# Pooled attention and two MLPs on one core: weights' signs taken by a parametric relu, key and value batches prepared in ten steps

## The chip, the cores and the metric

One core of one Trainium2 chip runs the whole kernel. The metric is the device time of one execution in microseconds (us). TensorE is called PE below, VectorE DVE, ScalarE ACT, GpSimd POOL, and SP is the queue of SyncE, which issues most DMAs. Each engine takes its instructions strictly in order.

## What is computed

```python
# q, k, v: (8, 8, 576, 64);  w_in: (512, 2048), w_out: (2048, 512), twice
k_p = k.reshape(B, H, 72, 8, D).mean(axis=3)
v_p = v.reshape(B, H, 72, 8, D).mean(axis=3)
scores = q @ k_p.T / sqrt(D)
attn = softmax(scores);  x = attn @ v_p            # 4608 tokens of 512
h = x @ moe_w_in                                    # MLP 1
g = where(h >= 1, h, where(h <= -1, 0, (h + 1)**2 / 4))
x = g @ moe_w_out
h = x @ moe2_w_in                                   # MLP 2
return (h * sigmoid(h)) @ moe2_w_out
```

The arrays come as 64-bit floats. The kernel reads them as pairs of 32-bit words (a low and a high word) and makes 32-bit floats of the weights itself.

## The kernel before

Products are made of float16 pairs (a high and a low half of each operand, three matmuls a product). The 4608 tokens are cut into nine token tiles of 512. MLP 1 runs tile by tile: 16 steps `s` in a tile, each with 12 matmuls for a chunk of h (`emit_h`), a chain on ACT and DVE that makes g (`pre_A`, `min_A`, `mid_A`, `post_A`, `split_g`), and the products with w_out (`yA`). MLP 2 runs afterwards, when all else is done.

Around this main loop there are four kinds of side work.

- **First attention.** The first 128-token blocks (0 to 3) are done in 32-bit floats before the main loop (`stages`); MLP 1 of token tile 0 can't start before.
- **Weights of MLP 1.** w_in comes in nine pieces of up to 256 columns (`weight_in`: `load`, `look`, `scales`, `work`), w_out in eight halves of four column blocks d (`weight_out`). A piece is looked at for its largest entry (`look`), gets a scale (`w_scale`), and is converted: the exponent bits are shifted by 3, the sign is put in, the low word's top bits are put in, it is multiplied by the scale, cut to float16, and the rest is made by a subtraction on POOL. In the kernel before, ACT's Abs with a factor 2^-112 makes the positive high word, one DVE instruction floors it and accumulates the maximum (L248, L190), one shifts (L93), one ORs the sign in (L267 for w_in, L202 for w_out), one ORs the low bits in (L270, L208). Tile 0 runs while its own weights are still being converted.
- **Weights of MLP 2** (`weight_whole`) are converted the same way during tiles 1 to 7.
- **Attention of the later blocks** runs in slots (`att_slots`), four for each block of 128 tokens: one or two slots a step. For each batch of 576 tokens keys and values are prepared: half of each is loaded through SP (`kv_load`), the other half is added by an accumulating DMA that POOL issues (`kv_more`), DVE adds the quarters (`kv_pool`, L459 and L462), ACT takes the mean magnitude (L465), then the sums are scaled, split, and the keys are transposed by two DMAs on SP (`kT<-rows`, L502). The queries of each block go through the same kind of tile (`rows`, two buffers) and a transposing DMA (`qT<-rows`, L554).

The instruction order of each engine is made by a scheduler that runs a model of the timeline; `tc.issue_after` and the helpers `behind` and `paced` hold work back behind an anchor instruction. In the kernel before the sums of a batch are spread evenly over the slots (`pool_to`), and `batches` makes keys and values in the slot of the block that needs them first.

## Time and profile before

| | us |
|---|---|
| median of 3 runs | 1641.39 (1640.28 to 1647.74) |
| the profiled execution | 1640.59 |
| its span, first to last instruction | 1638.8 |

Stretches by what runs in them, in us from the span's start (the boundaries are the first splits of tile 0's last block and the first stores of the outputs of tiles 0, 1, 3 and 8):

| stretch | what runs |
|---|---|
| 0 to 48.3 | first attention; w_in is loaded, its first pieces looked at |
| 48.3 to 134 | tile 0: h and g; w_in converted, the first column block of w_out converted |
| 134 to 209.5 | tile 0: products with w_out; the other three blocks of w_out converted; attention of tile 1 |
| 209.5 to 334.2 | tile 1, two attention slots a step at first |
| 334.2 to 525.7 | tiles 2 and 3 |
| 525.7 to 959.2 | tiles 4 to 8 |
| 959.2 to 1638.8 | MLP 2 |

A window's row gives the busy time of each engine in it, with the number of instructions, then the granted share of PE's clock, the mean share of the 16 DMA engines and their rate. A row of waits gives who waited for whom, the time in total, how often, and the longest. A row of a group gives line, engine, operation, names and shapes, count, then busy time and the mean duration in ns.

### The profile page before, as it was taken

Reading aid. Unit: us, or ns where it says so; the run is one execution under the profiler, and the core shown is the slowest. Engines: PE = TensorE matmul, PEld = TensorE weight load, DVE = VectorE, ACT = ScalarE, POOL = GpSimd, SP = SyncE. Lnnn points to the kernel's source line nnn. Section 1 sums busy time; section 2 is a strip of 40 time slices with the busy share of each in tenths; the row PEclk is TensorE's granted clock in tenths of the full one; section 3 lists DMA queues with packets and bytes.
Section 4 is the critical chain, followed back from the end, with each engine's and each line's share of the span. In section 5 each row is a group of like instructions: output and inputs, shape, how many; then the busy total and the mean of one; then the engine's idle time right before and its main releaser. Section 6 shows DMA issues by size and latency. Waiting matters only on the chain.

```text
span 1638.8 us, 34439 instructions
## 1 busy us (share of the span) xinstructions
PE 1534.5 (94%) x14278; PEld 1052.6 (64%) x14278; DVE 1208.5 (74%) x2166; ACT 894.1 (55%) x1418; POOL 581.8 (36%) x507
## 2 busy tenths in 40 slices
PE   6765889799999999999999999999999999999998
PEld 5322434344444444444444479999999999999998
DVE  6898868566777687787767767777776777777765
ACT  4477455455666556574566555554444544455543
POOL 2342513113343332331355424433333433343322
PEclk9876899899999999999999999999999999999999
DMA  9573688927547366255574330001100000000000
GB/s 295 123 181 86 122 165 190 186 73 130 145 107 166 89 111 138 81 140 163 194 302 145 148 129 28 27 27 32 36 27 28 27 34 34 27 27 28 27 15 27
DMA packets 226157, 166.35 MB, mean 102 GB/s; under 512 B 154960, under 2 KB 193616, under 8 KB 226000
## 3 DMA queue, kind: packets, MB, share of 16 engines
q1 hardware_dynamic: 216592, 155.88, 35.4%
q0 software_dynamic: 9408, 8.27, 3.7%
q8 instruction: 112, 1.84, 0.5%
q14 instruction: 45, 0.37, 0.1%
HBM read 102.76 MB, written 33.55 MB: 83 GB/s over the span
## 4 chain that ended last, share of the span: by engine, by line
PE 50%; DVE 16%; DMA 9%; issue 9%; ACT 9%; POOL 6%; SPq 1%; DVEq 0%; POOLq 0%; ACTq 0%
PE y L120 5%; PE y L122 5%; PE y L121 5%; PE hps L120 4%; PE hps L122 4%; PE hps L121 4%; PE y L1024 4%; PE y L1025 4%; PE y L1026 4%; PE hb L122 4%; PE hb L121 4%; PE hb L120 4%; POOL c L724 4%; DMA kT<-rows 3%; DMA yin<-y 2%
## 5 line engine op out<-in xcount | busy, mean ns | idle before, releaser
L121 PE MATMUL hb<-xl,wc 128*128 128x128 f16 x2016 | 347.6, 219 | 0.0
L122 PE MATMUL hb<-xh,wc 128*128 128x128 f16 x2016 | 347.6, 219 | 0.0
L120 PE MATMUL hb<-xh,wc 128*128 128x128 f16 x2016 | 347.6, 219 | 0.0
L368 DVE SCALAR_TENSOR_TENSOR g<-c,tsg,g 128x512 f16<-128x512 f32 x252 | 228.7, 910 | 97.8 <-ACT g L367 97.8
L1024 PE MATMUL y<-wd,g 128*128 128x256 f16 x1008 | 274.7, 273 | 1.9 <-DVE ob L1037 1.8
L1026 PE MATMUL y<-wd,g 128*128 128x256 f16 x1008 | 274.7, 273 | 0.0
L1025 PE MATMUL y<-wd,g 128*128 128x256 f16 x1008 | 274.7, 273 | 0.0
L120 PE MATMUL hps<-xh,wa 128*128 128x512 f16 x576 | 222.7, 387 | 36.2 <-ACT wa L275 19.7
L964 ACT ACTIVATE c<-c,tc 128x512 f32<-128x512 f32 x144 | 103.2, 717 | 230.8 <-DVE c L961 230.8
L367 ACT ACTIVATE g<-c,tsg 128x512 f16<-128x512 f32 x252 | 177.6, 718 | 85.8 <-POOL c L727 48.3
L122 PE MATMUL hps<-xh,wa 128*128 128x512 f16 x576 | 220.7, 384 | 3.8 <-POOL wa L276 3.8
L121 PE MATMUL hps<-xl,wa 128*128 128x512 f16 x576 | 222.8, 387 | 0.4 <-DVE xl L368 0.2
L120 PE MATMUL y<-g,wb 128*128 128x512 f16 x544 | 210.0, 388 | 11.6 <-ACT wb L220 9.8
L122 PE MATMUL y<-g,wb 128*128 128x512 f16 x544 | 210.6, 387 | 4.7 <-POOL wb L221 4.7
L121 PE MATMUL y<-g,wb 128*128 128x512 f16 x544 | 210.7, 387 | 0.5 <-DVE g L863 0.5
L121 PEld LDWEIGHTS <-wc 128*128 128x128 f16 x2016 | 197.3, 98 | 2.4
L120 PEld LDWEIGHTS <-wc 128*128 128x128 f16 x2016 | 197.3, 98 | 2.2
L122 PEld LDWEIGHTS <-wc 128*128 128x128 f16 x2016 | 197.3, 98 | 0.0
L961 DVE TENSOR_TENSOR c<-c,hb 128x512 f32<-128x512 f32 x252 | 167.8, 681 | 38.6 <-PE hb L122 36.2
L834 DVE SCALAR_TENSOR_TENSOR g<-g,tbr,u 128x512 f32<-128x512 f32 x144 | 126.4, 878 | 59.0 <-ACT u L830 58.1
L724 POOL TENSOR_TENSOR c<-c 128x512 f32<-128x512 f32 x108 | 164.0, 1533 | 2.8
L603 POOL TENSOR_TENSOR e<-e,den 128x576 f32<-128x576 f32 x36 | 49.6, 1378 | 313.6 <-DVE den L602 226.2
(185 smaller groups left out, 2710.3 us busy)
## 6 DMA issues: line engine op xcount, KB each, us to landing
raw<-in_moe_w_out_dram SPq DMA_DIRECT2D x21, 1024.0 KB
raw<-in_moe_w_in_dram SPq DMA_DIRECT2D x18, 1024.0 KB
y<-y SPq DMA_DIRECT2D x36, 256.0 KB
yin<-y SPq DMA_DIRECT2D x18, 512.0 KB
out_dram<-ob SPq DMA_DIRECT2D x36, 256.0 KB
d<-hl SPq DMA_DIRECT2D x32, 256.0 KB
qt<-in_q_dram SPq DMA_DIRECT2D x31, 256.0 KB
wc<-d SPq DMA_DIRECT2D x8, 896.0 KB
```

The costliest lines, as they stand in the source:

```text
L120: nc.tensor.matmul(out=acc, lhsT=wh, rhs=xh, start=start, stop=False)
L121: nc.tensor.matmul(out=acc, lhsT=wh, rhs=xl, start=False, stop=False)
L122: anchor["pe"] = nc.tensor.matmul(out=acc, lhsT=wl, rhs=xh, start=False, stop=stop)
L367: a = nc.scalar.activation(out=hi, in_=x, func=AF.Copy, scale=s)
L368: return a, nc.vector.scalar_tensor_tensor(out=lo, in0=x, scalar=s, in1=hi, op0=ALU.mult, op1=ALU.subtract)
L724: nc.gpsimd.tensor_tensor(out=out, in0=a, in1=b, op=ALU.subtract)
L834: anchor["dve"] = nc.vector.scalar_tensor_tensor(out=g32_t[s], in0=g32_t[s], scalar=r["br"], in1=u_t.pop(s), op0=ALU.subtract, op1=ALU.max)
L961: nc.vector.tensor_tensor(out=out, in0=x, in1=y, op=ALU.add)
L964: nc.scalar.activation(out=x, in_=x, func=AF.Silu, scale=r["c1"])
L1024: nc.tensor.matmul(out=acc, lhsT=xh, rhs=wh, start=start, stop=False)
L1025: nc.tensor.matmul(out=acc, lhsT=xh, rhs=wl, start=False, stop=False)
L1026: nc.tensor.matmul(out=acc, lhsT=xl, rhs=wh, start=False, stop=stop)
```

## The change

Four things are changed.

1. **Sign by parametric relu.** The conversion's first instruction is now ACT's `Prelu` of the high word, with a scale from a column, a bias column of -2^-126 and a slope of -2^32, in the place of the scaled Abs. It leaves the sign in the result, so the DVE instruction that ORs the sign in is gone from all pieces of all four weight matrices. It needs the scale of the piece, so it stands behind the look and the search for the scale. `w_scale` makes two factors of the maximum, in six small DVE instructions where there were two.
2. **Looks.** The maximum of a piece is taken by one `TENSOR_REDUCE` on DVE over the raw high words, without ACT. The looks at the nine w_in pieces, their scales and the conversions of pieces 1 and 2 are dealt over the steps of the first attention (`LOOKS`, `SCALES`). The first column block of w_out is looked at, searched and converted in steps 6 to 13 of tile 0 (`W2S`).
3. **Batches.** `pool_to` and `batches` are gone. For each batch ten calls stand at fixed slots ahead of the slot in which it is due (`PREP`), held behind anchors of five engines. Keys get buffers of their own (`krows`), and the mean of the sums is apart from the search for their scale, which follows two slots later.
4. **Small things.** The sums of the first batch's values move behind a later part of the first attention; `sum` has two buffers in the place of three; the small columns of a tile lie in one tile.

```diff
+    def w_scale(e, d, s, g, up=14):
+        ts(a, g, FLOOR_HIGH, DOWN, ALU.max, ALU.mult)
+        ts(b.bitcast(I32), a.bitcast(I32), EXP_MASK, op0=ALU.bitwise_and)
+        bits(d, b, -1.0, 15 + TOP)
+        ts(b.bitcast(I32), a.bitcast(I32), 0x00700000, 3, ALU.bitwise_and, ALU.logical_shift_left)
+        bits(s, b, -1.0, 254 - 8 * TOP + up)
+        ts(e.bitcast(I32), a.bitcast(I32), 0x7FF00000, 3, ALU.bitwise_and, ALU.logical_shift_left)
...
+    def signed(x, r, d):
+        nc.scalar.activation(out=x, in_=high(r, F32), func=AF.Prelu, scale=d, bias=under, alpha=-LIFT)
...
         def look(p):
-            x = room32(p)
-            nc.scalar.activation(out=x, in_=high(held[p], F32), func=AF.Abs, scale=DOWN)
-            nc.vector.tensor_scalar(
-                out=x, in0=x, scalar1=0.0, scalar2=FLOOR_DOWN, op0=ALU.max, op1=ALU.max, accum_out=mx[:, p:p + 1]
-            )
+            abs_max(mx[:, p:p + 1], high(held[p], F32))
...
-            ts(xi, room32(p).bitcast(I32), 3, op0=ALU.logical_shift_left)
-            nc.vector.scalar_tensor_tensor(
-                out=xi, in0=high(r, I32), scalar=-0x80000000, in1=xi, op0=ALU.bitwise_and, op1=ALU.bitwise_or
-            )
-            nc.vector.scalar_tensor_tensor(
-                out=xi, in0=low(r), scalar=29, in1=xi, op0=ALU.logical_shift_right, op1=ALU.bitwise_or
-            )
+            signed(x, r, down[:, p:p + 1])
+            shifted(x)
+            with_low(x, r)
...
+    def keys_mean(b):
+        krows[b] = [ap.tile([SPT, H, 2, D], F16, tag="krows", name="krows", bufs=2) for _ in range(2)]
+        sums_mean(sums[b, "k"], km, krows[b][0])
+
     def batch_keys(b):
-        x = sums.pop((b, "k"))
-        hi, lo = rows(SPT), rows(SPT)
-        s = sums_scale(x, km, ek[:, b:b + 1], hi)
-        split(hi[:, :, 0], lo[:, :, 0], x, s)
+        hi, lo = krows[b]
+        split(hi[:, :, 0], lo[:, :, 0], sums.pop((b, "k")), search(SPT, km, ek[:, b:b + 1]))
...
+    def due(b):
+        return 4 * (S * b // 128 - 2 * NI) - 3
+
+    PREP = [
+        (16, lambda b: kv_load(b, "k")), (15, lambda b: kv_load(b, "v")),
+        (13, lambda b: kv_more(b, "k")), (12, lambda b: kv_more(b, "v")),
+        (7, lambda b: sums_of(b, "k")), (6, lambda b: sums_of(b, "v")),
+        (5, lambda b: keys_mean(b)), (4, lambda b: values_mean(b)),
+        (3, lambda b: batch_keys(b)), (2, lambda b: batch_values(b)),
+    ]
+
+    def prepare(n):
+        for b in range(2, B):
+            for before, f in PREP:
+                if due(b) - before == n:
+                    with behind("pe", "act", "dve", "pool", "sp"):
+                        f(b)
...
+    LOOKS = {3: (1,), 4: (2, 3), 5: (4, 5), 6: (6, 7), 7: (8,)}
+    SCALES = {5: (1, 3), 6: (3, 6), 7: (6, 9)}
...
+        with behind("dve", "act", "pe"):
+            for p in LOOKS.get(n, ()):
+                look1(p)
+            if n in SCALES:
+                scales1(*SCALES[n])
+            if n in (5, 6):
+                convert1(n - 4)
...
-    for a, b in ((1, 3), (3, 7), (7, 9)):
-        for p in range(a, b):
-            if a > 1:
-                paced(lambda: look1(p), "x")
-            else:
-                look1(p)
-        scales1(a, b)
...
+    W2S = [6,7,9,10,11,13]
```

DVE where token tile 0 begins: `xl` is the low half of the last block of its input, `wa` are the tiles of w_in pieces, `xf` the 32-bit piece being converted. Before:

```order
L368 SCALAR_TENSOR_TENSOR xl<-att,tsv,xh 128x4x128
L248 TENSOR_SCALAR wa_131,cols<-wa_131 128x512
L248 TENSOR_SCALAR wa_132,cols<-wa_132 128x512
L248 TENSOR_SCALAR wa_133,cols<-wa_133 128x1024
L248 TENSOR_SCALAR wa_134,cols<-wa_134 128x1024
L248 TENSOR_SCALAR wa_135,cols<-wa_135 128x1024
L248 TENSOR_SCALAR wa_136,cols<-wa_136 128x1024
L93 TENSOR_SCALAR xf<-wa_129 128x1024
L93 TENSOR_SCALAR xf<-wa_130 128x1024
```

The same place now (line numbers of the changed kernel; L95 is the shift, L191 the low bits):

```order
L95 TENSOR_SCALAR xf<-xf 128x1024
L191 SCALAR_TENSOR_TENSOR xf<-raw,xf 128x1024
L95 TENSOR_SCALAR xf<-xf 128x1024
L251 TENSOR_REDUCE cols<-all 128x3
L350 SCALAR_TENSOR_TENSOR xl<-att,small,xh 128x4x128
L95 TENSOR_SCALAR xf<-xf 128x512
L191 SCALAR_TENSOR_TENSOR xf<-room,xf 128x1024
L97 TENSOR_SCALAR wt<-cols 128x3
L191 SCALAR_TENSOR_TENSOR xf<-room,xf 128x512
```

The six looks that stood behind the last split stand ahead of it, and so does the conversion of piece 1.

PE in tile 0, behind the matmuls of h with the last piece but one of w_in (`wa_135`; the last is `wa_136`). Before, the matmuls with the last piece follow:

```order
L122 LDWEIGHTS wa_135
L122 MATMUL hps<-xh,wa_135 128x512
L107 MATMUL all<-ident,cols 128x128
L120 LDWEIGHTS wa_136
L120 MATMUL hps<-xh,wa_136 128x512
```

Now (here `wa_136` is the last but one, and `wb_125` the first column block of w_out):

```order
L124 LDWEIGHTS wa_136
L124 MATMUL hps<-xh,wa_136 128x512
L109 MATMUL all<-ident,wm_741 128x128
L109 MATMUL all<-ident,cols 128x128
L122 LDWEIGHTS wb_125
L122 MATMUL y_1122<-g_609,wb_125 128x512
```

25 of the 48 matmuls with w_out's first column block now stand ahead of the first one with the last piece of w_in.

ACT where tile 1 begins; `sum` are the sums of a batch, `qt` the queries of a block. Before, the keys of batch 2 go into `rows` and the queries follow into the same two buffers:

```order
L367 ACTIVATE rows<-sum,skv 80x8x64
L367 ACTIVATE v_114<-sum,skv 72x512
L499 COPY rows<-rows 80x8x64 x2
L823 ACTIVATE g_1765<-hps,tbr,tc_1292 128x512
L830 ACTIVATE u<-u,trsg 128x512
L465 ACTIVATE rows,eq<-qt 128x512
```

Now the keys go into `krows`, ahead of the outputs of tile 0 (`y`):

```order
L349 ACTIVATE krows<-sum,skv 80x8x64
L448 ACTIVATE rows,eq<-qt 128x512
L487 COPY krows<-krows 80x8x64 x2
L349 ACTIVATE rows<-qt,sq 128x8x64
L349 ACTIVATE xh<-att,small 128x4x128
L889 ACTIVATE y_1751<-y_1122,cy 128x512
```

The queries no longer stand behind a buffer that the keys' transposes read.

## Rows read from the trace of the kernel before

**Rows 1.** Windows: PE, PEld, DVE, ACT, POOL busy; clock; DMA share, GB/s.

```profile
48.30:134.00 85.70, 53.45 (x217) 22.95 (x217) 82.06 (x128) 54.86 (x80) 34.26 (x19) 0.81 0.60 138
134.00:209.50 75.50, 57.95 (x398) 26.77 (x396) 60.60 (x126) 38.93 (x60) 29.47 (x20) 0.81 0.53 112
209.50:334.20 124.70, 106.08 (x670) 50.08 (x669) 86.71 (x209) 67.71 (x121) 27.55 (x27) 0.92 0.90 175
334.20:525.70 191.50, 185.62 (x1160) 88.22 (x1159) 134.29 (x277) 114.41 (x195) 63.95 (x62) 0.99 0.57 121
525.70:959.20 433.50, 428.27 (x2522) 202.17 (x2522) 316.61 (x548) 261.95 (x429) 164.02 (x159) 1.00 0.51 148
```

**Rows 2.** Waits of PE from 48.3 to 209.5 (total, times, longest).

```profile
PE hps L120 <- ACT wa L275: 19.7, 3, 9.4
PE y L120 <- ACT wb L220: 9.8, 3, 5.6
PE y L122 <- POOL wb L221: 4.7, 4, 1.6
PE hps L122 <- POOL wa L276: 3.8, 3, 2.3
```

**Rows 3.** Groups on DVE, 0 to 330, shapes apart (busy us, mean ns).

```profile
L111 DVE TENSOR_REDUCE cols<-raw 128x1 f32<-128x1024 f32 x8 | 9.7, 1211 | 0.0
L248 DVE TENSOR_SCALAR_CACHE_REDUCE wa<-wa 128x1024 f32<-128x1024 f32 x7 | 8.3, 1215 | 4.2 <-ACT wa L247 4.2
...
L202 DVE SCALAR_TENSOR_TENSOR xf<-raw,xf 128x1024 int32<-128x1024 int32 x5 | 6.9, 1388 | 0.1
...
L267 DVE SCALAR_TENSOR_TENSOR xf<-wb,xf 128x1024 int32<-128x1024 int32 x4 | 4.8, 1212 | 0.0
...
L93 DVE TENSOR_SCALAR xf<-wa 128x1024 int32<-128x1024 int32 x7 | 4.7, 685 | 0.0
L202 DVE SCALAR_TENSOR_TENSOR xf<-wb,xf 128x1024 int32<-128x1024 int32 x3 | 3.7, 1220 | 0.0
...
L267 DVE SCALAR_TENSOR_TENSOR xf<-room,xf 128x512 int32<-128x512 int32 x2 | 1.4, 684 | 0.0
...
L93 DVE TENSOR_SCALAR cols<-cols 128x1 int32<-128x1 int32 x8 | 1.1, 146 | 0.0
```

**Rows 4.** Groups on ACT, 0 to 330, shapes apart.

```profile
L823 ACT ACTIVATE g<-hps,tbr,tc 128x512 f32<-128x512 f32 x34 | 26.0, 768 | 3.8 <-PE hps L122 3.1 <-DVE stash L863 0.5
...
L185 ACT ACTIVATE xf<-raw 128x1024 f32<-128x1024 f32 x6 | 6.8, 1138 | 2.7 <-DMA raw<-in_moe_w_in_dram 2.1 <-POOL wb L221 0.6
```

**Rows 5.** Timeline: ACT's last look at w_in (start, us).

```profile
42.51 1.14 ACT L247 ACTIVATE wa<-wb 128x1024 f32<-128x1024 f32 x1
```

**Rows 6.** Timeline of PE: the wait for the last piece of w_in.

```profile
113.72 0.61 PE L120 MATMUL hps<-xh,wa 128*128 128x512 f16 x1 [9.25 <-ACT wa L275]
```

**Rows 7.** Waits from 209.5 to 334.2, ACT and PE.

```profile
ACT rows L465 <- DMA kT<-rows: 14.2, 3, 8.7
...
PE hps L120 <- ACT g L823: 10.0, 2, 6.8
...
PE att L564 <- DMA qT<-rows: 6.2, 1, 6.2
```

**Rows 8.** Timeline: ACT and PE at the longest of these waits.

```profile
224.38 0.63 ACT L465 ACTIVATE rows<-qt 128x512 f32<-128x512 f32 x1 [8.67 <-DMA kT<-rows]
...
225.82 0.59 PE L120 MATMUL hps<-xh,wa 128*128 128x512 f16 x1 [6.77 <-ACT g L823]
```

**Rows 9.** Waits of PE from 334.2 to 560.

```profile
PE hps L120 <- ACT g L823: 4.4, 3, 2.6
```

**Rows 10.** Chain that ended last, in order of time: keys' transposes; a matmul's step.

```profile
259.10 0.22 PE hps L120
...
279.53 20.89 DMA kT<-rows x2
```

**Rows 11.** DMA issues of POOL, 209.5 to 334.2: KB, median us to landing.

```profile
raw<-in_v_dram POOLq DMA_DIRECT2D x2, 512.0 KB, 14.7
```

## What the change will do to the time, predicted before it ran

> **What bounds the kernel now.** I read the windows by stage first, because the share of busy time over the whole span hides that the stages differ. From 525.7 to 959.2 PE is busy 428.3 of 433.5 us at full clock, and from 334.2 to 525.7 it is busy 185.6 of 191.5 [rows 1]: there the time is PE's, and nothing that the change takes from DVE or ACT can shorten it. MLP 2, behind 959.2, holds no edited work. What can be won lies between 48.3 and 334.2, with 4.4 us behind it.
>
> In the first part of tile 0 (48.3 to 134) DVE is busy 82.1 of 85.7 us, ACT 54.9 and PE 53.5 at a granted clock of 0.81 [rows 1]. PE's waits there, and in the next stretch, end on conversions of weights: 19.7 us on w_in's high halves, 3.8 on its low halves, 9.8 and 4.7 on w_out's [rows 2]. The conversions wait for DVE, which does looks, shifts, signs and low bits in front of the same tile's activation work. So in this part DVE sets the pace. From 134 to 209.5 DVE falls to 60.6 of 75.5 and PE has 58.0 [rows 1]; here the length of the chain look, scale, conversion counts as much as any engine's sum.
>
> In tile 1 (209.5 to 334.2) it is something else: DVE has 86.7 and ACT 67.7 of 124.7 us. ACT waits 14.2 us for the keys' transposes, since the next queries go into the buffers that these read; PE then waits 10.0 us for ACT's `pre_A`, and 6.2 us for a transpose of queries that were made late [rows 7]. One such place in order: ACT stands 8.67 us until 224.38, and PE stands 6.77 us until 225.82 [rows 8].
>
> **The change part by part.** The sum is made against the profiled execution, 1640.6 us (span 1638.8 and 1.8 around it); the median of the three runs is 0.8 above it.
>
> *Tile 0, first part (85.7 us).* DVE loses: the signs of w_in's pieces 1 to 8, six of 1.21 us and two of 0.68, 8.6 us; the two signs of w_out's first block at 1.39, 2.8; the looks at pieces 3 to 8, four of 1.22 and two of about 0.68 (taken as half a sign's width), 6.2, which move ahead of the last split of the first attention; the shift and the low bits of piece 1, 0.69 and 1.21 (taken as a sign's, the same form), 1.9, which move there too [rows 3]. It gains the longer `w_scale`: four more small instructions for w_out's first block and the six of the third w_in group, ten of 0.15, 1.5 [rows 3]. The w_out looks stay at 1.21 in either form [rows 3]. The sum is 8.6 + 2.8 + 6.2 + 1.9 - 1.5 = 18.0 us off DVE, so 64 us of work are left.
>
> Not all of it becomes time, since ACT gets the Prelus of pieces 4 to 8. The trace shows no Prelu. Its nearest row is the Abs of the same piece, 1.14 us; from below it is bounded by the same row, since it reads and writes as much, and from above by the Relu with two column operands, 0.77 us for half as many columns, twice that being 1.54 [rows 4]. I take 1.2, nearer to the Abs, which has the same shape. Four of full and one of half width are 5.4 us, so ACT has 60 (at 1.54: 62) in a part that could be 68 long. Two engines at nine tenths that feed each other will not both be full. I take 14 us of the 18, with 6 and 18 as ends.
>
> First the row: DVE is at 96% there and ACT at 64%, and the piece costs 1.14 on ACT and 1.21 to 1.39 on DVE [rows 1, 3, 4]. Against the move speaks the Trainium skill, "ScalarE: Activation LUTs", section "Rules for kernel authors": relu and max belong on VectorE and not on ScalarE, which it gives as up to about 3 times slower per element in bf16. By that rule the two kinds of sign, 11.4 us, would stay on DVE and the forecast would lie some 9 us higher; the trace disagrees with it for these 32-bit forms. The same page, section "Step-by-step: what each stage is for", states that an activation's throughput doesn't depend on the function, by which Prelu would cost what Abs does; no run shows that yet.
>
> *Tile 0, second part (75.5 us).* DVE loses the six signs of the other three blocks, 1.22 to 1.39 each, about 7.8 us, and gains twelve small instructions, 1.8 [rows 3]. It wasn't full here, so I count this at little. What counts is the order: 25 of the first block's 48 matmuls now stand ahead of the first matmul with the last piece of w_in, where PE stood 9.25 us [rows 6]. At 0.22 us from one to the next [rows 10] they are 5.5 us of work put into that wait. With 1.5 us for DVE's lighter load I take 7. The longer chain speaks against more: the Prelu now waits for the scale, where only the last multiplication did, so a late maximum delays everything behind it. Ends: 0 and 12.
>
> *Start of tile 0.* All looks now stand in DVE's queue ahead of the last split, and the last piece of w_in was looked at from 42.51 [rows 5]; splits, scales and the conversion of piece 1 stand behind that look. I take 1 us later, between 3 earlier (values' sums have moved out of the way on PE) and 4 later.
>
> *Tile 1 (124.7 us).* The keys have buffers of their own, so ACT no longer stops for their transposes, and the batch is ready slots ahead of its first use. All three waits of PE go: 10.0 + 6.2 = 16 us [rows 7]. What is late next is the transposes themselves: two took 20.9 us [rows 10], they are still on SP's queue, and the queries' and the attention's follow them there. For that the lower end is 4. The upper is 24: the clock is 0.92 here [rows 1], about 10 us lost, and most of the drops follow the waits.
>
> *Tiles 2 and 3.* PE's 4.4 us [rows 9] are the same wait of ACT; I take 4, between 0 and 5.
>
> *Costs nothing.* The 16 signs of MLP 2's weights and the Prelus in their place lie under PE at 99% [rows 1]; if PE weren't the bound there, they would be a gain. The small columns in one tile and the third `sum` buffer are used by work that stands in order anyway. Activation tables are loaded at the same two places in the new order, so Prelu brings no reload.
>
> Sum: 14 + 7 - 1 + 16 + 4 = 40. 1640.6 - 40 = 1600.6, with 0.8 for the median **1601 us**.
>
> **The rivals.**
> *ACT becomes the bound in tile 0.* For it: 60 to 62 us of ACT work in a chain with DVE, and Prelu unseen. Against it: the same work has 64% of the time now. First part 6, second 2, the rest as above: 6 + 2 - 1 + 16 + 4 = 27, 1614 us.
> *The transposes stay the brake in tile 1.* For it: 20.9 us for two of them and a DMA share of 0.90 [rows 1, 10]; PE takes its attention work in order. Against it: they now start slots earlier. Tile 1 gives 3, tiles 2 and 3 nothing: 14 + 7 - 1 + 3 = 23, 1618 us.
> *Slower: DVE stands for the second half of a batch.* The keys' sums come six slots behind the accumulating DMA of keys, and stand on DVE in front of tile work, whatever has landed. Such a DMA took 14.7 us to land [rows 11]; six slots are three steps in the first half of tile 1, where a step is 124.7/16 = 7.8 us, so about 23 us; later six steps. From 23 us on the sums wait in tile 1, and from about 35 later. The twelve waits of the six batches would have to be 6 us each to lose 72 us; that ends at 1601 + 72 = 1673. Against it: the 14.7.
> *Nothing comes of it.* The time that DVE loses in tile 0 comes back as waits elsewhere, and tile 1 waits for something new: 1640 us.
>
> **How the numbers follow.** Forecast 0.67, ACT 0.13, transposes 0.10, nothing 0.05, slower 0.05. The forecast's own range has the terms' better ends in part, 1580, and their worse ones in part, 1618. Of the rivals two lie at 1614 and 1618, so 1580 to 1626 leaves out some 2 in 10: the two last rivals, and a forecast whose terms all come out at one end. A measurement here can tell about 0.5%, 8 us. Faster by more than that: 0.88 (the first three cases but for their worst ends); within: 0.06; slower: 0.06.
>
> **What would show it.** In the new profile the first part of tile 0 should be some 72 us long with DVE and ACT both at 85 to 90%; Prelu should take 1.14 to 1.25 us; the waits of h on w_in's conversions should fall from 23.5 us to under 8; the wait before the last piece should be shorter by about the 5.5 us of moved matmuls; ACT should show no wait on the keys' transposes, and PE none over 3 us in tile 1; the first store of tile 0's outputs should come at about 189 in the place of 209.5, and that of tile 1 at about 298. From there on the distances should be those of before. It would be wrong if tile 0's gain were eaten by a later start, if tile 1 kept its 125 us with waits on transposed queries, or if DVE's longest waits were for landed halves of batches.

## The result, and the profile of the changed kernel

The changed kernel takes 1621.98 us (median of 4 runs, 1619.99 to 1622.98), the kernel before beside it 1640.84: a ratio of 0.9896 with a 95% interval of 0.9876 to 0.9916, 18.9 us less. I had forecast 40 us. The sign was right, and half of the gain is missing; the time lies near the slow end of the range that I gave, 1580 to 1626.

The two profiled executions are 1638.8 and 1618.2 us long. Each tile ends with the store of its first output, and the distances from store to store show where the 20.6 us came from:

| stretch | before | after | difference | forecast |
|---|---|---|---|---|
| start to the first h matmul | 48.3 | 59.9 | +11.5 | +1 |
| first h matmul to the last activation of tile 0 (its 16th step on DVE) | 97.5 | 84.2 | -13.2 | -14 |
| from there to tile 0's first store | 63.7 | 71.7 | +8.0 | -7 |
| tiles 1 to 4 | 402.1 | 377.3 | -24.8 | -20 |
| tiles 5 to 8 | 347.6 | 346.1 | -1.5 | 0 |
| behind the last tile's first store | 679.6 | 679.0 | -0.6 | 0 |

Tiles 1 to 4 are taken together because the number of h matmuls that a tile draws ahead differs between the kernels (between those stores both have nearly the same work). Tile 0 should have given 20 us and lost 6.3.

The windows of the changed kernel, by the same stages as [rows 1] (PE, PEld, DVE, ACT, POOL busy; clock; DMA share; GB/s):

```profile
59.85:134.00 74.15, 48.26 (x195) 20.63 (x195) 66.87 (x116) 60.35 (x86) 23.57 (x13) 0.78 0.43 112
134.00:215.80 81.80, 60.25 (x419) 28.00 (x418) 55.94 (x135) 45.54 (x71) 31.66 (x23) 0.81 0.75 137
215.80:325.90 110.10, 103.38 (x671) 49.92 (x671) 85.27 (x193) 63.52 (x111) 26.73 (x27) 0.97 0.93 179
325.90:502.50 176.60, 176.60 (x1131) 84.90 (x1129) 125.23 (x273) 112.11 (x191) 55.30 (x56) 1.00 0.63 125
502.50:939.20 436.70, 431.84 (x2540) 203.33 (x2538) 301.23 (x539) 264.86 (x429) 162.78 (x167) 1.00 0.58 152
```

The first two rows are cut at 134.00 as before; that is the same time and not the same event, so the table above, which cuts at events, is the one to go by. In the first part DVE is busy for 90% and ACT for 81% of 74 us, which is near the forecast. The second part is longer than before, with DVE down from 60.6 to 55.9 us and the DMA share up from 0.53 to 0.75. From 325.9 on PE is simply busy.

PE's waits in tile 0, which answer to [rows 2]:

```profile
PE y L122 <- ACT wb L220: 19.9, 2, 14.9
PE att L554 <- DVE xl L350: 8.3, 1, 8.3
PE all L109 <- DVE wm L95: 6.7, 1, 6.7
PE y L124 <- POOL wb L221: 3.6, 3, 1.7
...
PE hps L122 <- ACT wa L263: 1.8, 1, 1.8
```

The 23.5 us of waits of h on w_in's conversions are down to 3.0 (1.8 and 1.2), and so under the 8 forecast. But y stands 14.9 us in one piece for w_out's first block, the search for that block's largest weight takes 6.7, and an attention score 8.3. All of tile 0's waits behind its first h matmul came to 49.7 us before and come to 47.3 now. In order, PE at the place of [rows 6]:

```profile
102.40 0.38 PE L124 MATMUL hps<-xh,wa 128*128 128x512 f16 x1
109.45 0.80 PE L109 MATMUL all<-ident,wm 128*128 128x128 f32 x2 [6.66 <-DVE wm L95]
110.03 0.64 PE L109 MATMUL all<-ident,cols 128*128 128x128 f32 x2
125.58 0.61 PE L122 MATMUL y<-g,wb 128*128 128x512 f16 x1 [14.91 <-ACT wb L220]
```

The Prelu and DVE's steps, 0 to 330 us, shapes apart, which answer to [rows 3, 4]:

```profile
L183 ACT ACTIVATE xf<-raw,cols,ws 128x1024 f32<-128x1024 f32 x5 | 6.5, 1310 | 0.0
...
L183 ACT ACTIVATE xf<-room,cols 128x512 f32<-128x512 f32 x2 | 1.7, 848 | 0.0
```

The Abs on half a piece, before:

```profile
L247 ACT ACTIVATE wa<-room 128x512 f32<-128x512 f32 x2 | 1.3, 663 | 0.0
```

DVE's steps now:

```profile
L113 DVE TENSOR_REDUCE cols<-raw 128x1 f32<-128x1024 f32 x10 | 12.1, 1209 | 3.5 <-DMA raw<-in_moe_w_in_dram 3.5
L95 DVE TENSOR_SCALAR xf<-xf 128x1024 int32<-128x1024 int32 x15 | 10.2, 688 | 1.8 <-ACT xf L183 1.7
```

A Prelu is 1.31 us (forecast 1.2, between 1.14 and 1.54); the looks and shifts cost what they cost before. The Trainium skill, "ScalarE: Activation LUTs", section "Step-by-step: what each stage is for", has the throughput not depend on the function. The trace agrees: from 512 to 1024 columns Prelu grows from 0.85 to 1.31 us, and Abs (L247 before) from 0.66 to 1.14, so the further 512 columns cost 0.46 and 0.48. What Prelu costs more is some 0.17 to 0.19 us an instruction, whatever its length; whether that comes from the function or from its column operands no run tells.

Tile 1, the answer to [rows 7]: ACT's waits on the keys' transposes are gone, and PE waits 6.9 us where it had waited 18.6.

```profile
PE att L647 <- DMA aT<-e: 4.1, 1, 4.1
PE att L554 <- DVE xl L350: 1.6, 1, 1.6
PE hps L123 <- DVE xl L350: 1.2, 1, 1.2
```

```profile
ACT rows L448 <- DMA qT<-rows: 7.5, 3, 3.4
```

Nothing answers to [rows 9]: from 325.9 to 560 PE has no wait that the view lists.

Where did tile 0's gain go? Two views tell. The first is a window from 15.8 us, where DVE is done with the first sums, to the last activation of tile 0, in both kernels; before, then after:

```profile
15.80:145.80 130.00, 87.22 (x457) 47.01 (x458) 114.85 (x199) 84.58 (x124) 43.76 (x25) 0.83 0.67 173
```

```profile
15.80:144.10 128.30, 94.76 (x479) 57.40 (x479) 99.11 (x196) 83.36 (x121) 32.48 (x20) 0.85 0.62 165
```

DVE is busy for 15.7 us less, and the stretch is 1.7 us shorter: DVE is idle for 29.2 us in it where it was idle for 15.2. The second is SyncE's queue in the second part, which comes with e16 below.

### The profile page after: what moved, and what is told of

Same layout as the page of the kernel before. It is cut to its first block, busy times and chain, and to the rows that moved or that the text cites. A ratio compares the mean times of both kernels' runs of the same rounds, so it can differ in the third digit from the quotient of the medians.

```text
span 1618.2 us, 34378 instructions
## 1 busy us (share of the span) xinstructions
PE 1535.0 (95%) x14278; PEld 1060.2 (66%) x14278; DVE 1170.4 (72%) x2154; ACT 898.9 (56%) x1418; POOL 563.2 (35%) x508
## 4 chain that ended last, share of the span: by engine, by line
PE 56%; DVE 12%; issue 9%; ACT 8%; DMA 7%; POOL 7%; SPq 1%; DVEq 0%; POOLq 0%; ACTq 0%
PE y L122 6%; PE y L124 6%; PE y L123 6%; PE hps L123 5%; PE hps L124 5%; PE hps L122 5%; POOL c L714 4%; PE y L1018 3%; PE y L1020 3%; PE y L1019 3%; PE hb L123 3%; PE hb L122 3%; PE hb L124 3%; DMA yin<-y 3%; DVE g L350 2%
## 5 line engine op out<-in xcount | busy, mean ns | idle before, releaser
L350 DVE SCALAR_TENSOR_TENSOR g<-c,small,g 128x512 f16<-128x512 f32 x252 | 228.6, 910 | 94.4 <-ACT g L349 94.4
L958 ACT ACTIVATE c<-c,small 128x512 f32<-128x512 f32 x144 | 103.2, 717 | 230.4 <-DVE c L955 230.4
L349 ACT ACTIVATE g<-c,small 128x512 f16<-128x512 f32 x252 | 177.6, 718 | 85.7 <-POOL c L717 48.2
L828 DVE SCALAR_TENSOR_TENSOR g<-g,small,u 128x512 f32<-128x512 f32 x144 | 126.4, 878 | 61.8 <-ACT u L824 59.9
L593 POOL TENSOR_TENSOR e<-e,den 128x576 f32<-128x576 f32 x36 | 53.1, 1475 | 324.6 <-DVE den L592 234.5
```

The costliest lines, as they stand in the source:

```text
L349: a = nc.scalar.activation(out=hi, in_=x, func=AF.Copy, scale=s)
L350: return a, nc.vector.scalar_tensor_tensor(out=lo, in0=x, scalar=s, in1=hi, op0=ALU.mult, op1=ALU.subtract)
L828: anchor["dve"] = nc.vector.scalar_tensor_tensor(out=g32_t[s], in0=g32_t[s], scalar=r["br"], in1=u_t.pop(s), op0=ALU.subtract, op1=ALU.max)
L958: nc.scalar.activation(out=x, in_=x, func=AF.Silu, scale=r["c1"])
```

## The experiments

All ratios are to the kernel before, run beside them. The changed kernel stands at 0.9896 [0.9876, 0.9916].

### The start of tile 0

DVE's largest idle piece in the changed kernel lies ahead of the first h matmul. Its timeline there, and PE's:

```profile
42.93 0.46 DVE L568 TENSOR_REDUCE mx<-early 128x4 f32<-128x288 f32 x1 [6.94 <-PE early L559]
```

```profile
28.06 13.88 PE L434 MATMUL att<-v,ident 72*72 72x128 f32 x64
41.73 0.69 PE L559 MATMUL early<-k,qT 128*128 128x144 f32 x2
```

The 64 matmuls that sum the values stand in one run of 13.88 us ahead of the scores that DVE waits for. Before, the same 64 took half of that:

```profile
15.58 7.39 PE L451 MATMUL early<-v,ident 72*72 72x128 f32 x64
```

Their distance is 0.21 us here and 0.11 there, a ratio of two, as between the lower and the upper of PE's two levels (1.2 and 2.4 GHz). Here the level is read from the distances alone: the profile's granted clock reads 1.00 both in these 14 us and, in the kernel before, from 15 to 23 us. With the same 0.21 it reads 0.50 in e17 (28 to 42) and in e18 below, and in e19, with 0.11, 1.00. The last look at w_in, on ACT at 42.51 before [rows 5], is on DVE at 53.05, 10.5 us later, about as much as the first h matmul.

**e1: the sums back at their old place.**

```diff
         if n == 2:
+            sums_of(0, "v")
+            values_mean(0)
             look1(0)
...
-        if n == 3:
-            sums_of(0, "v")
-            values_mean(0)
```

> The changed kernel with one step moved back: the sums of the first batch's values (64 matmuls on PE) and their mean stand ahead of the first look, as before the change. Theory 'level': in the changed kernel PE runs the first attention at the lower of its two levels (those 64 matmuls stand 0.213 us apart, against 0.109 before), because its work there is sparser, and tile 0 begins 11.5 us late (59.85 against 48.34). It expects 0.11 us between these matmuls, the first matmul of h at 49 to 52 and a time of 1610 to 1614 us. Rival 'queue': tile 0 begins late because all looks stand in DVE's queue ahead of the last split; it expects the first h at 57 to 60 and 1619 to 1623 us.

Measured: 0.9878 [0.9847, 0.991]. The sums ran from 16.7 to 30.1, still at 0.21, and the first h matmul came at 58.83. So in this execution the old place didn't bring the old level.

**e7: 32 matmuls of the identity ahead of the first look**, to have PE busy before the sums.

```diff
         if n == 2:
+            warm = ps_h.tile([128, N], F32, tag="h", name="warm")
+            for _ in range(32):
+                nc.tensor.matmul(out=warm[:, 0:128], lhsT=ident, rhs=ident, start=True, stop=True)
             look1(0)
```

> The changed kernel with 32 matmuls of the identity more on PE ahead of the first look, whose result nobody reads; nothing else moves. Theory 'level': they cost PE some 4 to 7 us at 16 us, but lift it to the upper level; the values' matmuls stand 0.11 us apart, the first h comes at 50 to 56 and the time is 1611 to 1618 us. Theory 'queue' or 'place' (it matters where the values' sums stand, not how fast PE runs): the first h comes at 60 to 66 and the time is 1622 to 1628 us.

Measured: 0.9851 [0.9822, 0.988], first h matmul at 61.05, first store at 215.3; the sums at 0.21 again. But the added matmuls ran from 1.44 to 13.5 us, the later ones 0.11 us apart, and the sums came at 29.35. The eight score matmuls right behind the added ones took 1.15 us. Then PE stood 4.21 us for the queries' load, and eight such matmuls at 20.24 took 2.12. So the run doesn't show what a PE kept busy right up to the sums would do. The trace shows no gain in tile 0; that the median is some 5 us lower stays unexplained.

**e2: the looks at pieces 3 to 8 behind the first attention**, as before.

```diff
-    LOOKS = {3: (1,), 4: (2, 3), 5: (4, 5), 6: (6, 7), 7: (8,)}
-    SCALES = {5: (1, 3), 6: (3, 6), 7: (6, 9)}
+    LOOKS = {3: (1,), 4: (2,)}
+    SCALES = {5: (1, 3)}
...
+    for a, b in ((3, 7), (7, 9)):
+        for p in range(a, b):
+            paced(lambda: look1(p), "x")
+        scales1(a, b)
```

> The changed kernel with the looks at w_in's pieces 3 to 8 and their scales behind the first attention, as before the change; the values' sums stay late. Theory 'queue' expects the first h at 49 to 52 and 1610 to 1616 us. Theory 'level' expects PE still at the lower level, 0.21 us between the values' matmuls, the first h at 54 to 58, and a time of 1619 to 1628 us, since the looks come back into tile 0.

Measured: 0.9907 [0.9882, 0.9931]. The first h matmul came 4.3 us earlier, at 55.58, but the first store at 216.5 (215.8). DVE's work from 15.8 us to the last activation stayed the same (99.4 us, 99.1 in the changed kernel): the looks cost DVE as much on either side of the first h matmul, so an earlier first h alone is worth nothing.

**e11: three quarters of the sums left out.**

```diff
-            for n in range(POOL):
+            for n in range(POOL)[0::POOL - 1]:
```

> The changed kernel with 2 of the 8 steps of the first batch's value sums on TensorE (16 matmuls instead of 64); the other six steps are left out, so the values are not whole sums. It takes some 10 us off TensorE ahead of the first h matmul (the 64 matmuls stand 0.213 us apart). Theory 'start' (the first h matmul at 59.85 us instead of 48.34 is what the change loses in tile 0): first h matmul at 49 to 52 us, first store 8 to 10 us earlier than 215.8 us, total near 1612. Theory 'work' (VectorE's work up to the first y matmul binds; an earlier start only gives it back its idle 6.9 us at 36 to 43 us): first h matmul at 49 to 53, first y matmul 3 to 7 us earlier, first store 3 to 7 us earlier. Theory 'chain': first y matmul within 2 us of 125.6.

Measured: 0.9813 [0.9786, 0.9841], some 12 us better than the changed kernel. First h matmul 52.55, first store 204.5: 7.3 and 11.3 us earlier. DVE's idle 6.9 us are gone, and up to the last activation of tile 0 its idle time fell from 29.2 to 17.5 us. Time that DVE gets back here does reach the end.

**e17: the sums dealt between the scores.**

```diff
         for j, f in enumerate(stages):
+            if n == 4 and j == 4:
+                sums_of(0, "v")
+                values_mean(0)
             if 0 <= n - j < NI:
...
-        if n == 3:
-            sums_of(0, "v")
-            values_mean(0)
```

> The changed kernel with the first batch's value sums on TensorE written behind the scores of the fourth group of queries, ahead of the first product with the values, so that the scheduler deals them between the scores instead of in one run of 13.9 us. Nothing is left out. Theory 'start' (VectorE's idle 6.9 us at 36 to 43 us behind the run of sums is a loss that reaches the end): that idle time falls under 3 us, the first h matmul comes 2 to 6 us earlier than 59.85, the first store and the total as much. Theory 'level' (only the lower level of TensorE in this stretch costs; the sums take their 13.9 us wherever they stand): first h matmul within 2 us of 59.85, total 1618 to 1624.

Measured: 0.9888 [0.9873, 0.9903]. The idle piece of 6.94 became two of 2.37 and 3.68; first h matmul 58.71, first store 211.6. That lies between the two theories; in the time it can't be told from no change.

### Is it the order around w_out's first block?

**e3: all parts of that block in step 10.**

```diff
-        if s in W2S:
-            with behind("dve", "act", "pe"):
-                w2step(0, W2S.index(s))
+        if s == 10:
+            for n in range(6):
+                w2step(0, n)
```

> The changed kernel with the first column block of w_out looked at, searched and converted in one go in step 10, as before the change, in place of steps 6 to 13. Theory 'dealing': PE's waits of 6.7 us (the search's matmul) and 14.9 us (the block's products) come from the block's steps being dealt, since their instructions stand between others; it expects these two waits to fall to some 12 us together and 1611 to 1616 us. Rival 'chain': they come from the Prelu that has to wait for the scale, in whatever step it stands; it expects the waits to be 20 us or more together and 1620 to 1630 us.

Measured: 0.9875 [0.9848, 0.9901]. The 6.7 us wait is gone, the first y matmul comes at 123.0 with a wait of 16.6, the first store at 209.1, and tile 1's at 328.0 (325.9 in the changed kernel): what tile 0 won, tile 1 gave back.

**e10: w_out's Prelu freed from the search.** Its factor is a fixed column, so it no longer follows the data.

```diff
+        still = col()
+        nc.gpsimd.memset(still, 2.0 ** -97)
...
-            steps(lambda i=i: held.pop(i), lambda i=i: dst(i // 2, i % 2), lambda i=i: s[i // 2],
+            steps(lambda i=i: held.pop(i), lambda i=i: dst(i // 2, i % 2), lambda i=i: (still, s[i // 2][1]),
```

> The changed kernel, but for w_out the factor of the parametric relu is a fixed column (the search of each block is kept, its result goes only into the last scaling), so the relu of a w_out piece no longer waits for its block's search. Part of the computation is left out: the factor no longer follows the data. Theory 'chain' (tile 0 of the changed kernel ends late since look, search, relu, shift and low bits of the first w_out block now stand one behind the other): the first y matmul comes 5 to 10 us earlier than 125.6 us and the first store before 210 us. Theory 'work' (VectorE's total of work up to there sets the first y matmul, whatever the order): first y matmul within 2 us of 125.6, total 1617 to 1625.

Measured: 0.9871 [0.9845, 0.9896]. The wait didn't go; it stands in another place, 13.2 us ahead of an h matmul for w_in's last piece, the first y matmul came at 131.5 in place of 125.6, and the first store at 211.8. The longer chain (search, then Prelu) is not what holds tile 0.

**e12: y may not overtake h; e14: the block dealt earlier.**

```diff
-            yA(m, d, m == 0, m == KF - 1)
+            with behind("pe") if d == 0 and m == 0 else nullcontext():
+                yA(m, d, m == 0, m == KF - 1)
```

> The changed kernel, but the first y matmul of tile 0 may only be issued behind the last h matmul of tile 0 (in the changed kernel 25 h matmuls of tile 0 run behind it, while TensorE stands 14.9 us for the first w_out block). Theory 'order' (the wait for the w_in piece was turned into a wait for w_out because y was drawn ahead of h): the 14.9 us wait falls to under 8, since about 10 us of h run in it, and the first store comes 5 to 10 us earlier than 215.8. Theory 'work': the h matmuls cannot run earlier, since their accumulators come free only as VectorE gets to steps 13 to 15; the wait moves ahead of them, and the first store stays within 3 us.

```diff
-    W2S = [6,7,9,10,11,13]
+    W2S = [3,4,5,7,8,10]
```

> The changed kernel with the six parts of the first w_out block dealt at steps 3, 4, 5, 7, 8 and 10 instead of 6, 7, 9, 10, 11 and 13; no work is added or left out. Theory 'chain' or 'order' (the first y matmul waits for the block's long chain): first y matmul 10 us or more earlier than 125.6, its wait under 6 us, first store at 206 to 211. Theory 'work' (VectorE has the same work to do by then): the w_out block is ready earlier but the h accumulators come free later by as much; the y wait falls, waits ahead of h matmuls grow, and the first store stays within 3 us of 215.8.

Measured: 0.9872 [0.9842, 0.9901] and 0.9869 [0.9839, 0.9898]; first stores at 213.5 and 215.9. PE's longest waits in tile 0, of e12 and of e14:

```profile
PE hps L122 <- ACT wa L263: 20.9, 2, 19.1
PE y L122 <- ACT wb L220: 8.3, 3, 6.5
```

```profile
PE hps L122 <- ACT wa L263: 15.6, 2, 15.3
```

With y behind h the wait stands ahead of h and is 19.1 us; with w_out ready early it is again h, for 15.3. Whichever piece is put last is the one that PE waits for. The times of e3, e10, e12 and e14 can't be told from the changed kernel's. So the order inside the stretch is worth nothing that these runs can tell, and "work" holds of it: DVE was busy 25.7 of the 26 us from 100 to 126.

### What the removed signs are worth

**e5: the sign step once more on DVE**, in front of the low bits.

```diff
     def with_low(x, r):
         xi = x.bitcast(I32)
+        nc.vector.scalar_tensor_tensor(
+            out=xi, in0=high(r, I32), scalar=-0x80000000, in1=xi, op0=ALU.bitwise_and, op1=ALU.bitwise_or
+        )
```

> The changed kernel with the sign step on VectorE back in front of each low-bits step of the weights (a second OR of the sign that is there already, so the numbers stay the same): 1.2 us for each of the 40 odd pieces, 16 to 20 us of it in tile 0. Nothing is left out. Theory 'work' (VectorE's work sets tile 0): the first y matmul comes 8 to 13 us later than 125.6, total 1630 to 1638. Theory 'cover' (VectorE's work in tile 0 is no longer what binds, so its removal was worth little): first y matmul within 4 us of 125.6, total 1620 to 1627.

Measured: 0.9988 [0.9967, 1.0009], 1636.9 us: 15 us of the gain, nearly all of it, hang on the signs. The windows from 15.8 to the last activation of tile 0 and on to the first store:

```profile
15.80:150.60 134.80, 94.91 (x487) 55.55 (x487) 113.81 (x208) 84.41 (x121) 39.36 (x20) 0.78 0.60 157
150.60:226.60 76.00, 48.97 (x338) 22.47 (x337) 62.72 (x144) 41.39 (x64) 31.34 (x23) 0.80 0.80 142
```

14.7 us more work on DVE, 12.3 of them sign steps, made the first stretch 6.5 us longer and the second 4.3; another 4.6 us come in tile 8, where the last of MLP 2's weights are converted. The first y matmul came only 2.9 us later, less than "work" had said, since DVE's idle time shrank to 21.0 us: "work" has the sign and about half of the size.

### The third batch's loads

SyncE's queue in the changed kernel, second part of tile 0 (start, time to issue):

```profile
144.22 1.23 SPq L544 DMA_TRANSPOSE qT<-rows  x1
...
154.40 2.63 SPq L612 DMA_TRANSPOSE aT<-e  x2
157.15 1.56 SPq L410 DMA_DIRECT2D raw<-in_v_dram  x1
159.24 1.66 SPq L149 DMA_DIRECT2D raw<-in_moe_w_out_dram  x1
160.97 2.28 SPq L410 DMA_DIRECT2D raw<-in_v_dram  x1
163.36 4.91 SPq L544 DMA_TRANSPOSE qT<-rows  x1
168.32 0.58 SPq L521 DMA_DIRECT2D qt<-in_q_dram  x1
169.00 5.01 SPq L544 DMA_TRANSPOSE qT<-rows  x1
174.10 6.53 SPq L612 DMA_TRANSPOSE aT<-e  x2
```

A transpose of queries that is issued in 1.23 us ahead of the load of values takes 4.9 and 5.0 us behind it. Three of the third batch's four loads (the keys' second half, which GpSimd issues at 155.0, and both halves of the values, at 157.2 and 161.0 and on GpSimd at 168.7 and 172.2) now stand there together with w_out's last piece. In the kernel before all four were issued between 97 and 122, of which SyncE's:

```profile
97.07 1.18 SPq L426 DMA_DIRECT2D raw<-in_k_dram  x2
...
114.39 1.19 SPq L426 DMA_DIRECT2D raw<-in_v_dram  x2
```

What follows from the slow issues: ACT stands 6.09 us until 174.47 and 3.81 until 181.01 for queries' transposes, DVE behind it, and PE 8.32 until 183.61. From 170 to 180 DVE is busy 3.25 us of 10 (6.30 in e16).

**e16: these loads back in steps 10 to 13.**

```diff
-                if due(b) - before == n:
+                if due(b) - before == n and (b > 2 or before < 12):
...
+        if s == 10:
+            kv_load(2, "k")
+        if s == 12:
+            kv_more(2, "k")
+            kv_load(2, "v")
+        if s == 13:
+            kv_more(2, "v")
```

> The changed kernel with the four loads of the third batch (keys and values, first and second halves) issued in steps 10 to 13 of tile 0, about where the kernel before has them (97 to 122 us), instead of in the attention steps of the second part (155 to 173 us). Nothing is left out. Theory 'loads' (in the second part of tile 0 these loads meet the load of the last w_out piece and the transposes of the queries: SyncE's issues of those take 4 to 5 us each instead of 1.24, and TensorE stands 8.3 us at 183.6): the wait of 8.3 us falls to under 3, the transposes are issued in 1.3 us again, the stretch from the first y matmul to the first store falls from 90 to 80 to 84 us, the total to 1612 to 1616. Theory 'work' (VectorE's work alone bounds tile 0): the stretch keeps 88 us or more and the total 1618 to 1624.

Measured: 0.9842 [0.9826, 0.9859], 1611.7 us. Its queue:

```profile
156.88 0.52 SPq L149 DMA_DIRECT2D raw<-in_moe_w_out_dram  x1
157.58 2.42 SPq L544 DMA_TRANSPOSE qT<-rows  x1
...
167.54 1.29 SPq L544 DMA_TRANSPOSE qT<-rows  x1
```

The first store comes at 207.3 in place of 215.8, and from the last activation to it the stretch is 63.8 us, which is the 63.7 of the kernel before. Everything behind keeps its distances. Of the 8.0 us that the second part lost, 7.9 are these loads'. One number missed: the wait at the scores fell to 5.1, not under 3.

### Both losses together, and the sums on DVE

**e18: e16 with e17's sums. e19: e18 with e3's block.** No edits of their own.

> The changed kernel with both: the third batch's loads in steps 10 to 13 of tile 0, and the first batch's value sums dealt between the scores. Nothing is left out. If the two gains are separate (8 to 10 us by the loads; the sums moved the first store by 4 us but the total by no more than its noise): first store at 203 to 206 us, total 1606 to 1612. If the second is swallowed: first store at 207, total as with the loads alone, 1610 to 1614.

> As e18 (third batch's loads in steps 10 to 13, value sums dealt between the scores), and all six parts of the first w_out block in step 10 of tile 0, which alone brought the first store to 209.1 but the total no further than 1619.5. Nothing is left out. If VectorE's work sets the first part and the dealing inside it does not matter: first store at 203 to 208, total within 4 us of e18's 1608. If the block as a whole takes waits out: first store at 198 to 203, total 1602 to 1606.

Measured: 0.9816 [0.979, 0.9842] and 0.9824 [0.9802, 0.9845]; the medians are no different. The profiled executions differ: e18's took 1612.85 us, e19's 1604.23, while each kernel's own runs reach from 1603 to 1613. The order of instructions is the same in both up to the first h matmul. One run of 20 sums in e18, then in e19:

```profile
25.37 4.47 PE L434 MATMUL early<-v,ident 72*72 72x128 f32 x20
```

```profile
24.46 2.35 PE L434 MATMUL early<-v,ident 72*72 72x128 f32 x20
```

In e19's execution PE was at the upper level there (granted clock 1.00 from 24 to 30, in e18's 0.50 from 25 to 30), and the first h matmul came at 52.95 (60.33), the first store at 200.3 (207.3). So the level in this stretch isn't a property of the order: it differs between executions of the same instructions, and it is worth 7.4 us at the first h matmul. The 7.0 us at the first store can't be put down to it, since e3's block alone, in e3, brought that store forward by 6.7. Nor is it told whether the execution or the chip decides: e18 and e19 ran on two chips. Of the experiments that keep sums on PE, e19 and e22, both on one chip, show 0.11 us between them; all others, on four other chips, show 0.21.

**e22 and e23: half and all of the sums as reductions on DVE**, with e16's loads.

```diff
+            r = kv_raw[b, which, j // 2][:, j % 2 * 2:j % 2 * 2 + 2]
+            if j >= 0:
+                for h in range(2):
+                    nc.vector.tensor_reduce(
+                        out=sums[b, which][0:SP, 2 * j + h], in_=r[:, h].rearrange("p r d -> p d r"),
+                        axis=AX.X, op=ALU.add,
+                    )
+                return
             if j == 0:
                 kv_raw["ps"] = att_ps([SP, H, D])
-            ps, r = kv_raw["ps"], kv_raw[b, which, j // 2][:, j % 2 * 2:j % 2 * 2 + 2]
+            ps = kv_raw["ps"]
...
```

(In e22 the bound is 2, and the matmuls stay for the first half.)

> The changed kernel with the third batch's loads in steps 10 to 13 of tile 0 (as e16), and half of the first batch's value sums as four reductions on VectorE of about 1.0 us each (what the key sums take there) instead of 32 of the 64 matmuls, which take 6.9 us. Nothing is left out. Theory 'start' (the run of sums on TensorE holds VectorE idle for 6.9 us and so delays tile 0): first h matmul 2 to 5 us earlier than 59.4, first store 2 to 5 us earlier than 207.3, total 1607 to 1610. Theory 'VectorE's work': the four reductions cost as much as they free, first store within 2 us of 207.3, total 1610 to 1614.

> As e22 with all of the first batch's value sums on VectorE (eight reductions, about 8 us; TensorE's run of 13.9 us is gone). Nothing is left out. Theory 'start': first h matmul 4 to 8 us earlier than 59.4, first store 3 to 8 us earlier than 207.3, total 1604 to 1609. Theory 'VectorE's work': first h matmul earlier, but first store within 3 us of 207.3, total 1610 to 1614.

Measured: 0.9832 [0.9813, 0.9851] and 0.9787 [0.9763, 0.9811]. e22 is no better than e16: its first h matmul came at 51.49, its first store at 206.5; up to the last activation of tile 0 DVE's idle time fell by 8.1 us against e16, and its busy time rose by 7.3. The reductions are 4.0 of these 7.3. Two small steps that take 0.15 us elsewhere took 2.12 and 4.99 us, and both overlap subtractions on GpSimd; the longer one, and GpSimd's:

```profile
59.24 4.99 DVE L97 TENSOR_SCALAR cols<-wt 128x3 int32<-128x3 int32 x1
```

```profile
60.20 3.99 POOL L264 TENSOR_TENSOR wa<-xf,wa 128x1024 f16<-128x1024 f32 x2
```

So busy time isn't always work. In the traces of both kernels and of all the experiments, each DVE instruction between the first h matmul and the last activation of tile 0 that took over 0.3 us longer than the middle one of its kind overlaps an instruction on GpSimd. The surplus comes to 12.3 us before, 8.4 in the changed kernel and 13.0 in e22. Why they take longer was not tested.

e23 has the lowest median, 1606.5 us (runs from 1600.68 to 1607.49; its interval overlaps e18's). It has its first h matmul at 49.36 and its first store at 201.3. DVE's first sums and its window there:

```profile
15.77 3.77 DVE L433 TENSOR_REDUCE sum<-v 72x64 f32<-72x512 f32 x4 [4.45 <-DMA v<-in_v_dram]
```

```profile
15.80:131.30 115.50, 76.44 (x398) 41.11 (x399) 106.76 (x206) 83.32 (x120) 38.02 (x24) 0.79 0.82 198
```

DVE has 9.5 us more to do than in e16 (97.3 in 127.7 us) and is through 12.2 us earlier: its idle time is 8.7 us in place of 30.4. That speaks for "start": the sums' work on DVE cost less than DVE standing for PE. But it isn't a clean test. Of the 21.7 us less idle time 11.7 lie ahead of the first h matmul and 10.0 behind it, and there the order differs too: in e16 and e22 26 of the y matmuls run ahead of the last h matmul of tile 0, and DVE stands 4.4 and 5.4 us for that piece's h; in e23 only 2 do, and that wait is gone. e22, with 8.7 us less idle time ahead of the first h matmul, ended tile 0 only 0.8 us earlier. How much the start alone is worth stays open. What tile 0 still waits for in e23 is again the last conversions, 15.9 and 10.2 us; of the 12.2 us only 6.0 reach the first store.

### Tiles 1 to 4

**e4: keys and queries share two buffers again. e20: a batch's last four steps together. e21: both.**

```diff
-        krows[b] = [ap.tile([SPT, H, 2, D], F16, tag="krows", name="krows", bufs=2) for _ in range(2)]
+        krows[b] = [ap.tile([SPT, H, 2, D], F16, tag="rows", name="rows", bufs=2) for _ in range(2)]
```

```diff
-        (5, lambda b: keys_mean(b)), (4, lambda b: values_mean(b)),
-        (3, lambda b: batch_keys(b)), (2, lambda b: batch_values(b)),
+        (1, lambda b: keys_mean(b)), (1, lambda b: batch_keys(b)),
+        (1, lambda b: values_mean(b)), (1, lambda b: batch_values(b)),
```

> The changed kernel with the key rows back in the two buffers that the query rows use (one tag instead of two). Nothing is left out. Theory 'buffers' (ScalarE's waits on the key transposes in tiles 1 to 3, which the change ended, came from the shared buffers): the waits of ScalarE on the transposes come back, some 10 us each in tiles 1 to 3, the way from the first store to the fourth grows from 286.7 to 295 or more, total 1628 to 1638. Theory 'dealing' (it is the dealing of the preparation in ten steps that ended them): the way from the first store to the fourth stays within 4 us of 286.7, total 1618 to 1626.

> The changed kernel with the last four of the ten steps of each batch from the third on (both means, keys, values) written together, just ahead of the attention slot that needs them, about as the kernel before has them; the key rows keep their own buffers. Nothing is left out. Theory 'dealing' (the 29.5 us that tiles 1 to 3 gained came from these steps being dealt over four slots): TensorE's waits from the first to the fourth store rise from 6.9 to 15 us or more, that way grows from 286.7 to 300 or more, total 1630 or more. Theory 'buffers': the waits stay under 9 us and the way under 291, total 1619 to 1624, since the key rows no longer stand in the query rows' way.

> As e20, with the key rows also back in the query rows' buffers. Nothing is left out. Theory 'dealing': no worse than e20 by more than 4 us. Theory 'buffers': the waits of ScalarE on the key transposes come back (31.3 us from the first to the fourth store in the kernel before), the way from the first to the fourth store is 10 us or more above e20's. Theory 'either' (each of the two alone is enough to end these waits): e20 as the changed kernel, this one at 300 us or more.

| | ratio | first store | tiles 1 to 4 | PE's waits in them |
|---|---|---|---|---|
| before | | 209.5 | 402.1 | 24.6 |
| changed | 0.9896 [0.9876, 0.9916] | 215.8 | 377.3 | 6.9 |
| e4 | 0.9902 [0.9887, 0.9917] | 208.2 | 387.1 | 10.7 |
| e20 | 0.9901 [0.9883, 0.9918] | 211.3 | 379.1 | 8.0 |
| e21 | 0.9911 [0.9888, 0.9934] | 208.5 | 387.0 | 11.1 |

With shared buffers these tiles take 10 us longer, but tile 0 ends 7 us earlier, with less attention done ahead (18 more matmuls stand in tiles 1 to 4), so the time is the same. Dealing the last four steps is worth 2 us. ACT's waits on the keys' transposes, 31.3 us from 209 to 520 before, are 4.2 in e4 and 5.2 in e21. So neither of the two parts alone accounts for their end, nor do both: with both undone 15 of the 25 us remain. What is left of the change there, the earlier loads and sums and the lighter conversions, I didn't take apart; it stays open.

## Why the prediction was wrong

*What bounds the kernel.* Right where PE was full: from tile 5 on nothing moved by more than 1.5 us. Right also that DVE sets the pace in tile 0. But I let that begin at the first h matmul. It begins at 15.8 us: e2 brought the first h matmul forward by 4.3 us and the end of the tile not at all, since DVE's work was only moved, while e11 and e23, which took idle time off DVE ahead of it, moved the end (e23 by other things as well).

Two steps failed: the start of tile 0 came out 10.5 us worse than forecast, and its second part 15.0.

*Start of tile 0, +1: the first step that failed.* It took +11.5. From 15.8 to the first h matmul DVE has 28.8 us of work in place of 21.1, and stands idle 15.2 in place of 11.5. I had put 8.1 us of looks, shift and low bits there as if into free time, and wrote that the sums of the values had moved out of the way; they had moved into DVE's, as the 6.94 us until 42.93 show. How much of the 11.5 is the change's own can't be told wholly: the sums ran at the upper level in the one trace of before and at the lower in that of after, 6.5 us of difference, and e18 and e19 show that the same order of instructions can run at either.

*First part, -14.* -13.2 from the first h matmul to the last activation. The size is right, but not by the working: DVE's busy time fell by 23.4 us there (93.8 to 70.4), not 18, and its idle time grew by 10.2, for which I had allowed 4. Of the 23.4 some 3.9 are time that DVE's instructions took longer beside GpSimd's (12.3 us before, 8.4 now), which I had counted as work; and this stretch reaches to 145.8 before, while my 18 went to 134. So the nearness of -13.2 to -14 is in part luck. e5 puts the price on the signs themselves: 15 us of the time, in all tiles.

*Second part, -7: the second step that failed, and the larger.* It was +8.0, and two things failed. The 25 matmuls of y put ahead of w_in's last piece were worth nothing: y's own wait grew to 14.9 us, and with y held back it is h's, 19.1 (e12). And a part of the change that I had costed at nothing, the new place of the loads, costs 7.9 us there and 8.5 at the first store (e16). I had followed the ten steps for the sums and the rows of keys, and the DMAs only for the batches from tile 1 on; three of the third batch's loads had moved by some 40 to 50 us, in among w_out's last piece and the queries' transposes.

*Tiles 1 to 3, -20.* Tiles 1 to 4 gave 24.8: 17.7 us of waits, close to the 20 forecast, and some 7 us by which PE is busy for less time with nearly the same matmuls (377.6 us for 2383, 370.6 for 2379). The granted clock in tile 1 rose from 0.92 to 0.97 as the waits went. I had named that gain as the upper end and not taken it. That the buffers alone would do it was wrong (e4).

*The rivals.* ACT as the bound: no, 81% busy. The transposes as a brake: PE's longest wait in tile 1 is on one, but 4.1 us long; its time, 1618, came near the measured one by chance. DVE standing for landed halves: one wait of 1.88 us. The one that came true in part was "what DVE loses in tile 0 comes back as waits", for which I had written 0.05. It wasn't all or nothing: the start and the second part of tile 0 came out 25.5 us worse than forecast, the tiles behind it 6.9 better.

*The rule on relu* that the prediction weighed (the Trainium skill, "ScalarE: Activation LUTs", "Rules for kernel authors"), and held the trace to disagree with: it doesn't. The rule gives its figure for bf16 and for instructions with one source; DVE's sign step at 1.21 to 1.39 us has two. A 32-bit step with one source, the shift, takes 0.69 us on DVE, where Prelu takes 1.31 on ACT, so for such a step DVE is the faster here too. The sign was still better off on ACT, where an instruction on the same piece stood anyway, since DVE set the pace: e5 puts that at 15 us.

## What to carry to other kernels

When an engine sets the pace of a stage, look for where its queue was last empty, not for where the stage's first matmul stands: work moved in front of that matmul is only free if the engine stood idle there, and it must be counted against the idle pieces that are really left. When preparation is dealt into steps, follow every DMA of every step to the queue and the time at which it is now issued; a load that nobody waits for can still slow the issues behind it. If three different orders of a stretch give the same end, stop reordering and take work or idle time away. Before a fall in busy time is called work, look for instructions that take longer than others of their kind, and at what runs beside them.

## What the hardware showed unasked

PE's level in the first attention differs between executions of the same order of instructions: 20 matmuls took 2.35 us in one (granted clock 1.00) and 4.47 in another (0.50), worth 7.4 us at the first h matmul. What decides it was not found; the two ran on different chips, and e7's added matmuls ended over 15 us ahead of the sums, with a wait of 4.21 us between. SyncE's issue of a queries' transpose, 1.23 us ahead of the loads, took 4.9 to 5.0 us behind them, with a DMA share of 1.20 from 163 to 174; in e16, at 0.94 from 157 to 170, two of them took 2.42 and 1.29. Eight reductions on DVE at 1.0 us do in 8 us what 64 matmuls did in 13.88 at the lower level and 7.39 at the upper. And a DVE step on 128x3 elements, 0.15 us elsewhere, took 4.99 us beside GpSimd's subtractions.
